# Batch 0 of a fused attention and mixer kernel: half of k by plain fp32 DMA and pooled on VectorE, all of q by casting DMA, and a new written order

## The chip, the cores and the metric

The kernel runs on one core of one Trainium2 chip. The metric is device time in microseconds (us). A time that differs by less than about 0.5% can't be told from no change here.

Names used: PE is TensorE, PEld its weight loads, DVE is VectorE, ACT is ScalarE, POOL is GpSimd, SP is SyncE. PSUM is what PE writes to.

## The reference, cut to what matters

Inputs are q, k and v of 8 batches x 8 heads x 576 rows x 64, fp32, and four weights. Eight neighbouring rows of k and v are averaged to 72 rows ("pooling"). Then attention, then a mixer over tokens and one over channels:

```python
k_p = k.reshape(B, H, 72, 8, D).mean(axis=3);  v_p = (same of v)
attn = softmax(q @ k_p.T / sqrt(D));  x = attn @ v_p        # x: batch, 576, 512
h  = relu(x.T @ w_tok1) @ w_tok2;     u = x + h.T           # over tokens, 576 -> 256 -> 576
h2 = relu(u @ w_ch1) @ w_ch2;         out = u + h2          # over channels, 512 -> 1536 -> 512
```

The device works in bf16 with fp32 sums.

## The kernel before, in words

**Stages.** A "unit" is the channel mixer of 512 rows: unit n for batch n, and a ninth unit for the last 64 rows of all batches. First come 12 tiles of layer 1 (`l1_tile`, L517, four matmuls of 512 columns each, evicted through a relu by ACT, L521), then the layer 2 products (`product`, L583), which use sums of activations and of weights that DVE makes (`g_sums`, L545 and L557, and `weight_sum`). While unit n runs, the attention and the token mixer of later batches are put between its matmuls.

**Attention of a batch b >= 1.** k and v come in by casting DMA (fp32 to bf16) from POOL's queue (`kv`, L118), q likewise (L128). k is pooled by three adds (`pool8`, L174, L175, L178/L180), on POOL as step K0/K1 or on DVE as k0/k1, or by identity matmuls on PE (`kpool`, L253). `kpT` transposes pooled k on PE. `qD` (Q0, Q1; L284) transposes q in 32 x 32 blocks on DVE, two heads packed per word. `scores` (s0, s1, s2; L297) makes the scores in the four row quadrants of PE, ACT takes the exponentials (L306). v is pooled on POOL (V0, V1), on DVE (v0, v1) or on PE (`ppool`, vpool0/1, L264). `av` (L379) multiplies by v, DVE divides (L383, L384). `at` (L393) and `u` (L415, L416) are the token mixer, `t` or a trip through DRAM transposes u for layer 1.

**Batch 0** has its own code before: two of four head pairs of q come as fp32 by SP's hardware queue (L738) and are cast by ACT and DVE (step c0, c1, L690), the others by casting DMA; q is transposed on PE (`qT`, L275, L277); k is pooled on PE in three pieces (`kp2`, L232, L234), transposed (`kt2`, L243, L246); scores are taken per head pair with odd and even rows apart (`score`, steps o, e; L318, L322); `avh` (a00 ... a14; L333, L338, L339), `ath` (m00 ...; L356), `uT_x`, `uT_a` (X, A; L468, L476, L478) carry on. Matmuls on zeros (d2, d3 ...; L679) stand before and between.

**What sets the order.** Nothing is scheduled by a planner when the kernel is built: the program order of each engine is the order in which the Python code runs. `HEAD` is the list of steps before unit 0. `PLAN[n]` gives for each half tile of unit n (index 0 to 44) the steps that follow it. Each engine works through its own list in order, and waits where its next instruction needs something. A "g" in the plan is `gate` (L712, L713): DVE writes a flag and POOL copies it, so that POOL's later work starts no earlier than that place in DVE's list. POOL's casting DMAs run one after another on one queue, and an issue waits while the eighth DMA before it has not landed.

PSUM: four banks for single tiles (p1a to p1d, `take`/`give`), and two double banks (p2, shown as p).

Of the kernel before, what the change touches and what calls it, by code (L numbers as in the profile page):

```python
# [8 lines left out]
FP32 = mybir.dt.float32  # L9
# [11 lines left out]
HEAD = """LkA LkT LkB LvT Lq LvA LvB Lt1 Lk1 Lt2 Lc1b Lc1a Lq1 Lc1c Lv1 Lc1d p1 Lc2a Lc2b Lc2c d2 d2 d3 d1 d4 d4 c0 c1 prep q0 kp0 kp1 kt0 q1 d1 o0 kt1 kp2 e0 e1 q3 kt2 o1 q2 e3 vpool0 o3 e2 a00 vpool1 a02 o2 m01 d1 d1 m00 a04 X1 m03 a14 m02 X0 m04 p0 a10 a12 1.kpool m10 m14 m12 m13 m11 A1 A0 X2 X3 A2 A3"""  # L21
PLAN = [
# [13 lines left out]
def kernel(  # L36
# [18 lines left out]
    BOUNCED = range(3, B)  # L55
    SP = S // POOL
    BP, BR = 64, S // 64
    NE = (BR + 1) // 2
    EV, OD = NE * BP, (BR - NE) * BP
# [37 lines left out]
    qf = area2[:, 0:4 * BR * D].bitcast(FP32).rearrange("p (a n) -> p a n", a=2)  # L97
# [89 lines left out]
    def batch_steps(b):  # L187
# [5 lines left out]
        def prepare():  # L193
            kp = att.tile([SP, 2, 2, 4, D // 2], BF16, name="kp") if b >= 1 else None
            st.update(kp=kp, vp=values[par], ex=exps[par], xt=rests[b // 2 % 2])
            if not first:
                st["kD"] = att.tile([P, 2, 2, SP], BF16, name="kD")
# [15 lines left out]
        def pool(eng, t, g):  # L213
            def go():
                hs = slice(g * HP, (g + 1) * HP)
                pool8(eng, loaded[b, t], hs, st["kp"][:, g] if t == "k" else st["vp"][:, hs, 0:D], t == "k")
            return go
# [9 lines left out]
        def kp2(h0, h1):  # L227
            def go():
                ps = take([P, 512], FP32)
                n = (h1 - h0) * D  # L230
                for i in range(POOL):
                    nc.tensor.matmul(out=ps[0:SP, 0:n], lhsT=ident[0:SP, 0:SP], rhs=loaded[b, "k"][:, h0:h1, i, :],  # L232
                                     start=(i == 0), stop=(i == POOL - 1))
                nc.vector.tensor_copy(out=kpz[:, h0:h1, 1, :], in_=ps[0:SP, 0:n].rearrange("j (h d) -> j h d", d=D))  # L234
                give(ps)
            return go

        def kt2(h0, h1):
            def go():
                ps = take([P, 2, h1 - h0, SP], BF16)  # L240
                for odd in range(2):
                    for h in range(h0, h1):
                        nc.tensor.transpose(out=ps[:, odd, h - h0, :],  # L243
                                            in_=kpz[:, h, 1 - odd:3 - odd].rearrange("j e d -> j (e d)"),
                                            identity=ident[0:SP, 0:SP])
                nc.vector.tensor_copy(out=kT[:, :, h0 * SP:h1 * SP], in_=ps.rearrange("m o h j -> m o (h j)"))  # L246
                give(ps)
            return go
# [22 lines left out]
        def qT(hp):  # L271
            def go():
                ps = take([P, NE, 2, BP], BF16)
                for rr in range(NE):
                    nc.tensor.transpose(out=ps[:, rr].rearrange("m l p -> m (l p)"),  # L275
                                        in_=loaded[b, "q"][:, hp, rr * P:(rr + 1) * P], identity=ident)
                nc.vector.tensor_copy(out=qT0[:, hp].rearrange("m l (r p) -> m r l p", p=BP), in_=ps)  # L277
                give(ps)
            return go

# [8 lines left out]
        def scores(i):  # L289
            def go():  # L290
                pss = [ps_two.tile([P, 2, 512], FP32, name="p2") for _ in range(2)]
                spans = [(i, 0, 0, S1)] if i < 2 else [(g, g * (S - S1), S1, S) for g in range(2)]
                for g, o, n0, n1 in spans:
                    for db in range(2):
                        for l in range(4):
                            quad = slice(l * 32, (l + 1) * 32)
                            nc.tensor.matmul(out=pss[l // 2][0:SP, l % 2, o:o + n1 - n0], lhsT=st["kD"][quad, g, db, :],  # L297
# [3 lines left out]
                for a in range(2):  # L301
                    if i < 2:
                        dst, src = exv[:, a, :, i, 0:S1], pss[a][0:SP, :, 0:S1]
                    else:
                        dst, src = exv[:, a, :, :, S1:S], pss[a][0:SP, :, 0:2 * (S - S1)].rearrange("j l (g n) -> j l g n", g=2)
                    nc.scalar.activation(out=dst, in_=src, func=AF.Exp, scale=scale)  # L306
            return go

        def score(hp, odd):
            n = OD if odd else EV  # L310

            def go():
                ps = ps_two.tile([P, 2, 512], FP32, name="p2")
                exv = st["ex"][:, 0:H * S].rearrange("j (h n) -> j h n", h=H)[:, 2 * hp:2 * hp + 2]
                for hl in range(2):
                    h = 2 * hp + hl
# [466 lines left out]
```

## Time and profile before

| what | us |
|---|---|
| median of 3 runs | 266.4 (266.19 to 267.63) |
| span of the profiled execution, its only time on the page | 264.4 |
| median less span | 2.0 |
| PE busy | 256.2 (97%) |
| DVE, ACT, POOL busy | 178.4, 119.6, 153.1 |
| first score matmul of batch 0 (L318) | at 9.74 |
| first product with v (L333) | at 15.16 |
| first layer 1 matmul (L517) | at 24.60 |

The page divides the span into 40 slices and gives each engine's busy share in tenths. The timeline gives the start, duration, engine, line and operation of each instruction, in order. "x8" is eight instructions in a row, whose duration is from the first's start to the last's end. A wait is put down to what ended it.

### The profile page before, as it was taken

How to read it: one execution, taken by the hardware profiler on the slowest of the kernel's cores; microseconds unless marked ns; L12 is line 12 of the kernel's file. 1: busy time of each engine (PE TensorE's matmuls, PEld its weight loads, DVE VectorE, ACT ScalarE, POOL GpSimd, SP SyncE). 2: the span in 40 equal slices, each digit the busy share in tenths (PEclk: the TensorE clock that was granted, in tenths of full speed). 3: DMA queues.
4: the chain of work that ended last, by engine and by line, in shares of the span. 5: the costliest groups of instructions: out<-in, count | busy, mean ns of one | idle time of the engine just before them, and what ended most of it. 6: DMA issues, size and time to landing. Idle time of an engine off the chain costs nothing.

```text
span 264.4 us, 5328 instructions
## 1 busy us (share of the span) xinstructions
PE 256.2 (97%) x2121; PEld 160.3 (61%) x2121; DVE 178.4 (67%) x370; ACT 119.6 (45%) x195; POOL 153.1 (58%) x177
## 2 busy tenths in 40 slices
PE   8799999989999999999999999999999999999994
PEld 3685466744677545774487447744874486486483
DVE  3557569996787655895599678844795576184183
ACT  2355763149536456425641575165435412612700
POOL 8577326899999999988959982898200010100000
PEclk9999999999999999999999999999999999999999
DMA  6999999993088928699447940830513053404104
GB/s 141 193 195 206 205 207 208 205 216 80 4 129 141 166 82 171 149 202 266 91 132 107 232 144 17 158 94 4 159 38 122 30 170 80 121 0 102 59 0 159
DMA packets 31704, 34.29 MB, mean 130 GB/s; under 512 B 3136, under 2 KB 23744, under 8 KB 31680
## 3 DMA queue, kind: packets, MB, share of 16 engines
q0 software_dynamic: 17632, 17.64, 42.3%
q1 hardware_dynamic: 13632, 15.93, 20.2%
q10 hardware_dynamic: 416, 0.39, 0.5%
q8 instruction: 16, 0.26, 0.4%
q14 instruction: 8, 0.07, 0.1%
HBM read 38.99 MB, written 12.58 MB: 195 GB/s over the span
## 4 chain that ended last, share of the span: by engine, by line
PE 73%; DVE 12%; POOL 8%; issue 3%; DMA 2%; ACT 1%; POOLq 0%; ACTq 0%
PE p1c L517 10%; PE p1b L517 8%; PE p1a L517 7%; PE p1d L517 7%; PE p1d L583 6%; PE p1c L583 5%; PE p1b L583 4%; PE p1a L583 4%; POOL t L174 3%; PE p L297 3%; DVE x L384 3%; DVE area L545 3%; PE p L379 2%; DMA kr<-in_k_dram 2%; POOL t L175 2%
## 5 line engine op out<-in xcount | busy, mean ns | idle before, releaser
L517 PEld LDWEIGHTS <-w_ch 128*128 128x128 bf16 x432 | 39.5, 98 | 44.4 <-issue 2.7
L713 POOL COPY flag<-flag 1x1 f32<-1x1 f32 x47 | 15.3, 326 | 86.0 <-DVE flag L712 86.0
L583 PEld LDWEIGHTS <-area 128*128 128x128 bf16 x432 | 41.4, 98 | 7.8 <-issue 1.2
L306 ACT ACTIVATE ex<-p 72x768 bf16<-72x768 f32 x42 | 31.6, 803 | 17.1 <-PE p L297 17.1
L583 PEld LDWEIGHTS <-GT 128*128 128x128 bf16 x324 | 30.7, 98 | 7.9 <-issue 1.6
L175 POOL TENSOR_TENSOR t<-t 72x512 f32<-72x512 f32 x23 | 31.2, 1358 | 1.8
L517 PE MATMUL p1c<-uT,w_ch 128*128 128x512 bf16 x116 | 31.4, 379 | 0.0
L521 ACT ACTIVATE GT<-p1b 128x512 bf16<-128x512 f32 x27 | 16.1, 597 | 27.5 <-PE p1b L517 20.9
L521 ACT ACTIVATE GT<-p1c 128x512 bf16<-128x512 f32 x32 | 19.1, 598 | 15.5 <-PE p1c L517 11.7
L517 PE MATMUL p1b<-uT,w_ch 128*128 128x512 bf16 x96 | 26.0, 379 | 0.0
L174 POOL TENSOR_TENSOR t<-kr 72x1024 f32<-72x1024 bf16 x12 | 25.5, 2121 | 0.4
L174 POOL TENSOR_TENSOR t<-vr 72x1024 f32<-72x1024 bf16 x11 | 23.4, 2125 | 1.0 <-DMA vr<-in_v_dram 0.5
L517 PE MATMUL p1a<-uT,w_ch 128*128 128x512 bf16 x88 | 23.9, 379 | 0.0
L517 PE MATMUL p1d<-uT,w_ch 128*128 128x512 bf16 x84 | 22.2, 379 | 0.0
L521 ACT ACTIVATE GT<-p1a 128x512 bf16<-128x512 f32 x25 | 14.9, 597 | 15.4 <-PE p1a L517 14.8
L521 ACT ACTIVATE GT<-p1d 128x512 bf16<-128x512 f32 x24 | 14.4, 599 | 12.8 <-PE p1d L517 7.3
L384 DVE TENSOR_TENSOR x<-p,den 128x512 bf16<-128x512 f32 x28 | 19.3, 691 | 1.0
L545 DVE TENSOR_TENSOR area<-GT 128x1536 bf16<-128x1536 bf16 x9 | 11.3, 1257 | 11.9 <-ACT GT L521 6.7
L557 DVE TENSOR_TENSOR area<-GT 128x1536 bf16<-128x1536 bf16 x9 | 9.5, 1054 | 11.3 <-ACT GT L521 11.3
L379 PEld LDWEIGHTS <-ex 72*128 72x128 bf16 x280 | 12.9, 98 | 6.5 <-DVE x L384 1.4
L379 PE MATMUL p<-vp,ex 72*128 72x65 bf16 x280 | 14.4, 194 | 0.3 <-POOL vp L180 0.2
L118 POOL DMA_DIRECT2D kr<-in_k_dram x17 | 10.9, 646 | 5.6 <-PE p1b L222 1.9
(185 smaller groups left out, 464.2 us busy)
## 6 DMA issues: line engine op xcount, KB each, us to landing
out_dram<-o SPq DMA_DIRECT2D x32, 256.0 KB, 4.2
qb<-in_q_dram POOLq DMA_DIRECT2D x7, 576.0 KB, 9.4
kr<-in_k_dram POOLq DMA_DIRECT2D x7, 512.0 KB, 8.4
vr<-in_v_dram POOLq DMA_DIRECT2D x7, 512.0 KB, 14.0
w_ch<-in_moe_w_ch_dram POOLq DMA_DIRECT2D x5, 512.0 KB, 14.8
mem<-u SPq DMA_DIRECT2D x10, 256.0 KB, 2.2
v<-mem SPq DMA_DIRECT2D x20, 128.0 KB, 2.9
area<-in_q_dram SPq DMA_DIRECT2D x2, 288.0 KB, 3.0
```

Source lines behind the costliest of these rows:

```text
L118: nc.gpsimd.dma_start(out=t[j0:j1, h0:h1].rearrange("j h i d -> j h (i d)"), in_=src[b, h0:h1].rearrange("h (j i) d -> j h (i d)", i=POOL) ...
L174: eng.tensor_tensor(out=t4[:, 0:n], in0=t[:, hs, 0:4], in1=t[:, hs, 4:8], op=ALU.add)
L175: eng.tensor_tensor(out=t4[:, 0:n, 0:2], in0=t4[:, 0:n, 0:2], in1=t4[:, 0:n, 2:4], op=ALU.add)
L306: nc.scalar.activation(out=dst, in_=src, func=AF.Exp, scale=scale)
L379: nc.tensor.matmul(out=ps[:, h // 4, (h % 4) * (D + 1):(h % 4 + 1) * (D + 1)], lhsT=st["ex"][:, h * S + n0:h * S + n0 + P], rhs=st["vp"][: ...
L384: nc.vector.tensor_tensor(out=dst.rearrange("p (a h d) -> p a h d", a=2, d=D), in0=view[:, :, :, 0:D], in1=den[rows, :, :, None].broadcast ...
L517: nc.tensor.matmul(out=ps, lhsT=w_ch1[:, kk, m * P:(m + 1) * P], rhs=uT[kk], start=(kk == 0), stop=(kk == 3))
L521: nc.scalar.activation(out=GT[:, m, :], in_=ps, func=AF.Relu)
L545: nc.vector.tensor_tensor(out=out, in0=a, in1=b, op=ALU.subtract)
L557: nc.vector.tensor_tensor(out=S4[:, 0], in0=GT[:, f, hi], in1=GT[:, sec, hi], op=ALU.add)
L583: nc.tensor.matmul(out=ps[i] if split else ps[:, i], lhsT=chunk(u, i, a(m)), rhs=w(m), start=start and m == 0 and (i == 0 or split), stop= ...
L713: nc.gpsimd.tensor_copy(out=flag[:, 1:2], in_=flag[:, 0:1])
```

## The change

- k of batch 0: heads 0 to 3 come as fp32 by the hardware queues (64 rows of the 72 from SP, 8 from ACT) into `kf`, and are pooled by three adds on DVE (step k0). Heads 4 to 7 come by casting DMA and are pooled on PE (kp1), as before but in one piece. Both are written in the layout of the other batches, transposed by two PE transposes each (`kt2`) and copied by DVE.
- q of batch 0: all by casting DMA, in two pieces of four heads, in the layout of the other batches, and transposed on DVE (Q0, Q1). `qT`, `score`, the casts c0 and c1 and the zero matmuls go. The scores are those of the other batches (s0, s1, s2).
- v of batch 0, heads 0 to 3: pooled on DVE (v0) where PE did it (vpool0); the same for batch 1. In later units four POOL steps become DVE steps: 5.K0, 6.K0, 7.V1 and 7.V0.
- `HEAD` and `PLAN` are written anew: order of the DMAs and of all steps, places of the gates. The pooling of batch 2's k loses the gate between its halves, and the transposes of that (2.kpT) go from index 44 of unit 0 to index 0 of unit 1. 0.u0 goes from unit 0 to the head.

```diff
-HEAD = """LkA LkT LkB LvT Lq LvA LvB Lt1 Lk1 Lt2 Lc1b Lc1a Lq1 Lc1c Lv1 Lc1d p1 Lc2a Lc2b Lc2c d2 d2 d3 d1 d4 d4 c0 c1 prep q0 kp0 kp1 kt0 q1 d1 o0 kt1 kp2 e0 e1 q3 kt2 o1 q2 e3 vpool0 o3 e2 a00 vpool1 a02 o2 m01 d1 d1 m00 a04 X1 m03 a14 m02 X0 m04 p0 a10 a12 1.kpool m10 m14 m12 m13 m11 A1 A0 X2 X3 A2 A3"""
+HEAD = """LkT LkB Lq0 LvT Lq+ LvA LvB Lt1 Lt2 Lk1 Lc1a prep Lq1 k0 Lc1b Lc1c Lv1 p1 kt0 Lc1d Lc2a Lc2b Q0 kp1 Q1 s0 kt1 s1 s2 v0 vpool1 Lc2c a00 a02 a04 p0 m01 a10 X0 X1 m02 a14 m04 m03 m00 a12 m14 m10 m11 A0 A1 m12 X3 m13 1.kpool X2 A3 A2 0.u0 1.Q1"""
-    {0: "2.lk 0.u1 1.kpT 1.Q0 1.Q1", 3: "0.u0 3.lq 2.lq", 6: "1.s0 0.u2", 8: "g", 9: "0.u3 1.s1", 10: "1.vpool1 2.lv", 12: "1.s2 1.vpool0", 13: "=3", 14: "1.av1 1.av2", 17: "1.av0", 18: "1.av4 g", 19: "w0", 20: "3.lv 1.av3", 22: "w1", 23: "g =1 =2", 24: "3.lk", 25: "=4", 26: "1.at0 g", 27: "2.K0", 28: "w3 1.at1", 30: "g", 31: "1.u2", 32: "2.K1", 33: "1.u0 2.V0", 34: "1.u1", 35: "w2", 37: "1.t2", 40: "1.u3", 41: "1.t0", 42: "1.t3", 43: "1.t1 2.Q0 1.u4", 44: "g 2.kpT 2.Q1 3.Q0"},
+    {0: "1.kpT g", 3: "2.lk", 4: "1.Q0 2.lq", 5: "1.s0", 6: "g", 7: "0.u2", 8: "1.v0 1.s1", 12: "1.s2", 13: "=3 1.vpool1 2.lv", 14: "3.lq g 3.lk 0.u1 1.av2", 16: "1.av1", 17: "1.av0 0.u3", 18: "1.av4", 20: "3.lv w0", 22: "1.av3 w1", 24: "1.at1", 25: "=1", 26: "=2", 27: "1.at0 =4", 28: "g 2.K0", 29: "2.K1", 30: "1.u0 g w3", 31: "1.u2", 33: "1.u1 2.V0", 34: "w2", 37: "1.t2", 39: "1.u3", 40: "1.t1", 42: "1.t0 2.Q0 1.t3", 43: "1.u4 2.Q1 g", 44: "3.Q0"},
...
+    kf = area[0:SP, 0:4096].bitcast(FP32).rearrange("j (l i d) -> j l i d", l=HP, i=POOL)
...
+        def kt2(g):
+            def go():
+                ps = take([P, 2, SP], BF16)
+                for e in range(2):
+                    nc.tensor.transpose(out=ps[:, e, :], in_=st["kp"][:, g, e].rearrange("j l d -> j (l d)"),
+                                        identity=ident[0:SP, 0:SP])
+                nc.vector.tensor_copy(out=st["kD"][:, g], in_=ps)
...
-    def late_q():
-        nc.gpsimd.dma_start(out=loaded[0, "q"][:, 2:HP, 0:BR * D], in_=q_pairs(2, HP))
+    def first_q(g):
+        if (0, "q") not in loaded:
+            loaded[0, "q"] = raw.tile([P, HP, BR * D + D], BF16, name="qb")
+        nc.gpsimd.dma_start(out=quarters(loaded[0, "q"])[:, g],
+                            in_=q[0, g * HP:(g + 1) * HP].rearrange("l (j n) d -> (l j) (n d)", n=2 * BR))
...
+        for j0, j1 in ((0, BP), (BP, SP)):
+            (nc.scalar if j0 else nc.sync).dma_start(out=kf[j0:j1].rearrange("j l i d -> j l (i d)"),
+                                                     in_=k[0, 0:HP].rearrange("h (j i) d -> j h (i d)", i=POOL)[j0:j1])
```

More of the change, by code (lines that the diff above doesn't have):

```diff
@@ L54 @@
     POOL = 8
-    BOUNCED = range(3, B)
+    BOUNCED = [b for b in range(B) if any(f"{b}.M" in t.split() for at in PLAN for t in at.values())]
     SP = S // POOL
     BP, BR = 64, S // 64
-    NE = (BR + 1) // 2
-    EV, OD = NE * BP, (BR - NE) * BP
     S1 = 3 * P
@@ L193, in prepare @@
         def prepare():
[L194 to L197, printed above, removed]
+            st["kp"] = att.tile([SP, 2, 2, 4, D // 2], BF16, name="kp")
+            st["kD"] = att.tile([P, 2, 2, SP], BF16, name="kD")
+            st.update(vp=values[par], ex=exps[par], xt=rests[b // 2 % 2])
         def late(key):
@@ L215, in go @@
                 hs = slice(g * HP, (g + 1) * HP)
-                pool8(eng, loaded[b, t], hs, st["kp"][:, g] if t == "k" else st["vp"][:, hs, 0:D], t == "k")
+                pool8(eng, kf if first and t == "k" else loaded[b, t], hs, st["kp"][:, g] if t == "k" else st["vp"][:, hs, 0:D], t == "k")
             return go
@@ L225, in kpT, with kp2 @@
             give(ps)
-        def kp2(h0, h1):
+        def kp2(g):
             def go():
                 ps = take([P, 512], FP32)
-                n = (h1 - h0) * D
+                hs = slice(g * HP, (g + 1) * HP)
                 for i in range(POOL):
-                    nc.tensor.matmul(out=ps[0:SP, 0:n], lhsT=ident[0:SP, 0:SP], rhs=loaded[b, "k"][:, h0:h1, i, :],
+                    nc.tensor.matmul(out=ps[0:SP, 0:HP * D], lhsT=ident[0:SP, 0:SP], rhs=loaded[b, "k"][:, hs, i, :],
                                      start=(i == 0), stop=(i == POOL - 1))
-                nc.vector.tensor_copy(out=kpz[:, h0:h1, 1, :], in_=ps[0:SP, 0:n].rearrange("j (h d) -> j h d", d=D))
+                nc.vector.tensor_copy(out=st["kp"][:, g].rearrange("j e l d -> j e (l d)"),
+                                      in_=ps[0:SP, 0:HP * D].rearrange("j (n e) -> j e n", e=2))
                 give(ps)
             return go
-        def kt2(h0, h1):
+        def kt2(g):
             def go():
[L240 to L246, printed above, removed]
+                ps = take([P, 2, SP], BF16)
[3 more added lines that the diff above has]
+                nc.vector.tensor_copy(out=st["kD"][:, g], in_=ps)
                 give(ps)
@@ L269, in ppool @@
             return go
[L271 to L279, printed above, removed]
         def qD(g):
@@ L287, in qD, with scores @@
             return go
-        def scores(i):
+        def scores(spans):
+            n = spans[0][2] - spans[0][1]
             def go():
                 pss = [ps_two.tile([P, 2, 512], FP32, name="p2") for _ in range(2)]
-                spans = [(i, 0, 0, S1)] if i < 2 else [(g, g * (S - S1), S1, S) for g in range(2)]
-                for g, o, n0, n1 in spans:
+                for i, (g, n0, n1) in enumerate(spans):
+                    o = i * n
                     for db in range(2):
@@ L296, in go @@
                             quad = slice(l * 32, (l + 1) * 32)
[L297 removed]
+                            nc.tensor.matmul(out=pss[l // 2][0:SP, l % 2, o:o + n], lhsT=st["kD"][quad, g, db, :],
                                              rhs=st["qD"][quad, g, n0:n1, db], start=(db == 0 and o == 0),
@@ L301, in go @@
                 for a in range(2):
-                    if i < 2:
-                        dst, src = exv[:, a, :, i, 0:S1], pss[a][0:SP, :, 0:S1]
+                    g, n0, n1 = spans[0]
+                    if len(spans) == 1:
+                        dst, src = exv[:, a, :, g, n0:n1], pss[a][0:SP, :, 0:n]
                     else:
-                        dst, src = exv[:, a, :, :, S1:S], pss[a][0:SP, :, 0:2 * (S - S1)].rearrange("j l (g n) -> j l g n", g=2)
+                        dst, src = exv[:, a, :, :, n0:n1], pss[a][0:SP, :, 0:2 * n].rearrange("j l (g n) -> j l g n", g=2)
                     nc.scalar.activation(out=dst, in_=src, func=AF.Exp, scale=scale)
[L307 to L316, printed above, removed]
-                    keys = slice(h * SP, (h + 1) * SP)
-                    nc.tensor.matmul(out=ps[0:SP, hl, 0:n], lhsT=kT[:, odd, keys], rhs=qT0[:, hp, hl, 0:n],
-                                     start=True, stop=True)
-                dst = exv.rearrange("j h (r p) -> j h r p", p=BP)[:, :, odd:BR:2, :]
-                src = ps[0:SP, :, 0:n].rearrange("j h (r p) -> j h r p", p=BP)
-                nc.scalar.activation(out=dst, in_=src, func=AF.Exp, scale=scale)
             return go
@@ L487, in batch_steps @@
                 name[t + str(g)] = pool(nc.vector, t, g)
-        for hp in range(HP):
-            if hp < 3:
-                hs = ((0, 2), (2, 4), (4, 8))[hp]
-                name[f"kp{hp}"], name[f"kt{hp}"] = kp2(*hs), kt2(*hs)
-            name[f"q{hp}"], name[f"o{hp}"], name[f"e{hp}"] = qT(hp), score(hp, 1), score(hp, 0)
-        for i in range(3):
-            name[f"s{i}"] = scores(i)
+        for g in range(2):
+            name[f"kp{g}"], name[f"kt{g}"] = kp2(g), kt2(g)
+            name[f"s{g}"], name[f"S{g}"], name[f"f{g}"] = (scores([(g, *r)]) for r in ((0, S1), (0, 512), (S1, S)))
+        name["s2"], name["S2"] = (scores([(g, n, S) for g in range(2)]) for n in (S1, 512))
         for c in range(5):
@@ L687, in head @@
             batches[1][0]()
-        elif s[0] == "c":
-            a = int(s[1:])
-            (nc.vector.tensor_copy if a % 2 else nc.scalar.copy)(out=loaded[0, "q"][:, a, 0:BR * D], in_=qf[:, a, :])
         else:
@@ L750 @@
             head(s)
-        for n in range(B + 1):
-            unit(n, PLAN[n])
+        for n, at in enumerate(PLAN):
+            unit(n, at)
 _INS = ['q', 'k', 'v', 'moe_w_tok1', 'moe_w_tok2', 'moe_w_ch1', 'moe_w_ch2']
```

15 lines of the change are left out of this document (2 added, 13 removed), and 16 rows, old and new, of the table PLAN.

## The prediction

> **What bounds the kernel now.** I read the page's busy line and slices first, then the busy time by stretches of 6 us, PE's waits, and the timeline of the head.
>
> ```profile
> PE 256.2 (97%) x2121; PEld 160.3 (61%) x2121; DVE 178.4 (67%) x370; ACT 119.6 (45%) x195; POOL 153.1 (58%) x177
> PE   8799999989999999999999999999999999999994
> POOL 8577326899999999988959982898200010100000
> ```
>
> PE is busy in nearly every slice after the fourth. POOL is full from slice 8 to about 20, then nearly idle. The stretches (columns: PE, PEld, DVE, ACT, POOL, then clock, DMA share, GB/s) say the same:
>
> ```profile
> 0.00:6.00 6.00, 4.81 (x15) 1.88 (x16) 2.51 (x11) 1.95 (x2) 4.89 (x13) 1.00 0.67 144
> 24.00:30.00 6.00, 6.00 (x38) 2.60 (x37) 3.72 (x7) 3.50 (x7) 1.29 (x2) 1.00 1.23 205
> 54.00:60.00 6.00, 5.08 (x47) 2.75 (x45) 5.54 (x10) 3.46 (x7) 5.69 (x5) 1.00 1.14 220
> 132.00:204.00 72.00, 71.80 (x632) 45.36 (x625) 54.19 (x117) 33.08 (x54) 43.45 (x46) 1.00 0.46 112
> ```
>
> From 24 us PE loses only 0.9 at 54 to 60, 0.3 at 84 to 96, 0.2 at 138 to 144 and the tail. PE's waits name the first two:
>
> ```profile
> PE p1c L222 <- POOL kp L178: 0.9, 1, 0.9
> PE p L379 <- POOL vp L180: 0.2, 1, 0.2
> ```
>
> So the time is: start of the first L517, plus PE's work from there (239.8 us with its waits). A change counts only as it moves that start, PE's later work, or a later PE wait. The head, from the timeline:
>
> ```profile
> 8.04 0.61 PE L232 MATMUL p1d<-kr,ident 72*72 72x128 bf16 x8 [1.30 <-DMA kr<-in_k_dram]
> 15.16 0.41 PE L333 MATMUL p<-vp,ex 72*128 72x65 bf16 x8 [0.41 <-ACT ex L322]
> 24.60 0.59 PE L517 MATMUL p1c<-uT,w_ch 128*128 128x512 bf16 x2
> ```
>
> PE waits for k's DMA, then for exponentials, and is full from 15.16 on.
>
> **A: PE's work after the first L517.** vpool0 of batch 1 goes: eight matmuls start at 34.65 and the next work at 35.55, so 0.9. 0.u0 moves ahead of it: 26.89 to 27.32, 0.4. Together -1.3. No other count on PE changes there.
>
> **B: the start of the first L517.** Landings of the old casting DMAs, from the DMA view narrowed to single issues, by KB queued in total: 256 at 6.65, 320 at 7.9, 576 at 9.3, 640 at 10.2, 928 at 11.25, 1184 at 12.65, 1440 at 13.9. The new queue holds kT, kB (288), q0 (576), vT (640), q+ (928), vA (1184), vB (1440): the same total beside the same fp32 bytes (576 KB by hardware, which landed by 4.3). So I take: kB 7.3, q0 9.3, q+ 11.25, vA 12.65, vB 13.9. The loads ahead of batch 1's v also sum to the same, so that lands at 31.5 as now. ACT issues one small DMA ahead of its table load (1.28 us): hidden, since its first exponential comes after 10.
>
> - k0 on DVE, from 4.3. Nearest rows are the three adds of 2.v1: 1.52, 1.64 and 0.84, 4.1 us from 59.21 to 63.29, beside a busy POOL. POOL only issues DMAs here. Low end: a DVE add from PSUM of 512 columns takes 0.68, so 1024, 512 and 256 columns are about 1.2, 0.65 and 0.4, 2.2 in all. k0 is done by 6.5 to 8.4, kt0 by 7.1 to 9.0. q0 covers either.
> - kp1: eight 256-column matmuls from 7.3, 0.9 (1.8 at half rate): hidden by q0 too.
> - Q0: 9.3 + 0.76 (row L284) = 10.05. s0 to its first exponential is 0.57 (28.71 to 29.28): 10.6. Two exponentials take 1.5: 12.1. Q1: 11.25 + 0.76 = 12.0; behind it in DVE's list stands kt1's copy, 0.3: 12.3. s1 0.57: 12.9 to 14.4. s2 about 0.45: 14.85 to 16.35.
> - v0 on DVE: 12.65 + 2.2 = 14.9, hidden (with 4.1, 16.75, 0.9 too late). vpool1 on PE: 14.9 to 15.8, and a00 follows at 15.8 where the product now starts at 15.16.
> - From a00 the division chain on DVE sets the pace: four at 0.9 and two at 0.6 from 16.3 reach 21.1. Then PE does m12, X3, m13 (0.22 each), 1.kpool 1.73, X2 0.22, A3, A2 and 0.u0 (0.43 each): 3.9. First L517 at 25.0, so +0.4. w_tok2 lands earlier (about 17 for 19.8) and is not in the way.
>
> **C: waits in unit 0.** v0 of batch 1 is new on DVE and waits for the landing at 31.5. Behind it stand =3 (0.9), vpool1's cast (0.35), u1 and the divisions. v0 ends at 33.8 (2.2; POOL again issues DMAs only) and the cast at 35.1. PE reaches av2 at 25.0 + 9.8 = 34.8: 15 half tiles of 0.432 are 6.5, and kpT, s0, u2, s1, s2, vpool1 and u1 are 3.3. A new wait of 0.3; with 4.1 for v0 it is 2.2.
>
> On goes DVE's list from 33.8: =3, the cast, three u and s of 0.65, five divisions of 0.9, w0, w1, =1, =2, =4 of 0.95: 12.4, the gate at 46.2. POOL's copy 0.8, then 2.K0 and 2.K1 of 4.35 each (47.87 to 52.2 now) without the flag of 0.9 between: 55.9. PE reached 2.kpT at 56.4 and now does at 56.4 + 0.4 + 0.3 - 1.3 + 0.4 (one index later) = 56.2. The wait of 0.9 goes, with 0.3 to spare: -0.9. POOL and PE are then both 1.6 ahead, so 3.K1 and batch 3's V meet PE as now.
>
> **D: four half poolings from POOL to DVE in units 3 to 5.** POOL's relief is worth nothing: no PE wait after 100 names it. DVE was busy 54.2 of 72 us there. Four times 2.2 fits in the idle 17.8; four times 4.1 just fills it. Low end 0, or -0.2 if a wait on DVE goes by the new order; high end 4 (below). PE lost only 0.2 where DVE was busy 5.8 of 6 (138 to 144), so I take +0.3.
>
> **Sum.** 264.4 - 1.3 + 0.4 + 0.3 - 0.9 + 0.3 = 263.2 of span. The median stood 2.0 above the span: 265.2.
>
> **The clock, row and rule.** The zero matmuls go, and with them what keeps PE busy early:
>
> ```profile
> 2.87 1.49 PE L679 MATMUL p1c<-area 128*128 128x512 bf16 x3
> 4.57 1.03 PE L679 MATMUL p1a<-area 128*128 128x512 bf16 x4
> ```
>
> Three take 1.49 (0.43 apart), later four take 1.03 (0.217 apart): half rate until 4.5, after 3.3 us of unbroken matmuls. Now PE starts near 7 with 1.8 us of kp1, then short pieces with gaps until 14.9. The trace has no row for that. I take full rate by s1.
>
> The Trainium skill, "TensorE: Matmul & The Clock Gate", section "Part 1: The HAM clock gate", says that half rate is the default and that about 3.4 us of sustained matmuls lift it; this trace's rows agree. Read strictly it would give the first rival's time.
>
> **Rivals.**
>
> 1. *Half rate lasts into the a-steps.* For it: no 3.3 us stretch before 14.9. Against: PE was broken up from 6.9 to 8.0 too and stayed fast. s0, s1 and s2 cost about 0.25 each, vpool1 1.8 for 0.9: a00 at 17.4. The 4.3 us of PE work up to m12 has 5.2 of division chain as cover; with 3 us of it at half rate it is 5.8, so +0.5. First L517 at 27.1: 264.4 + 2.5 - 1.3 - 0.9 + 0.3 (C's new wait gone, PE being late) = 265.0, so 267.0.
> 2. *DVE becomes the bound in units 3 to 5* (slower than before). Place: the eviction of u, or a division, behind 5.k0, 6.k0, 7.v1, 7.v0. Each holds DVE for up to 4.1; PE has other PSUM banks for three tiles of 0.87, 2.6. From there on PE waits: 1.5 for each of the first two, and with 7.v1 and 7.v0 close together (=3 between) 1 more: 263.2 - 0.3 + 4 = 266.9, so 268.9. For it: 4.1 is the only row of DVE pooling. Against: POOL was busy only 1.2 of the 26 us from 186, so the last two run alone and would be near 2.2.
>
> The Trainium skill, "GPSIMD Engine Reference", section "1. Specifications", says that the two engines share SBUF interfaces, with contention at DVE instructions of two SBUF inputs, as these adds are. The 1.64 of row L175, against 0.65 by columns, agrees.
>
> 3. *More waits go.* Batch 3's V (0.2), the three waits on divisions (0.2, 0.2, 0.4) and the tail's on s (0.3) end too, and D costs nothing: 262.9 - 1.2 = 261.7, so 263.7. For it: =3 is moved ahead in the last unit, POOL has less to do. Against: those on DVE are of one engine that gets more work.
>
> **How the numbers follow.** Chances: forecast 0.45, clock 0.25, DVE 0.17, more waits gone 0.13. The forecast's own range is 264.3 to 266.3 (v0's price and D). The range of 8 in 10 takes in the clock rival, the third, and the DVE rival where it costs up to 3 of its 4: 263.5 to 268.0. With the bounds of 0.5% at 265.07 and 267.73: faster 0.22 + 0.04 + 0 + 0.13 = 0.39; slower 0.02 + 0.04 + 0.12 = 0.18; same 0.43.
>
> **What would show it.** B: first L481 (the new line of L517) at 25.0, a00's product (L300) at 15.8, Q0 at 9.3. A row of 0.43 apart for 512 columns, or 0.213 for 256, after 12 us speaks for rival 1. C: av2's first product (new L345) waiting for vp about 0.3, and no PE wait for POOL's kp near 56. D: new PE waits for DVE between 130 and 215. What would make it wrong: q0's DMA not keeping the place in the queue that its bytes give it; 64 KB on eight partitions took 1.25 us before, and half of that now stands first.

## The result: 4.8% slower

The kernel after takes 279.14 us (median of four, 277.15 to 281.17), the kernel before 266.29 beside it: a ratio of 1.048, 95% interval 1.042 to 1.053. Forecast were 265.2 and a range up to 268.0. The profiled execution has a span of 277.1 (before 264.4), so 12.7 us are to be found.

The busy line and the slices of the page, after:

```profile
PE 252.6 (91%) x2029; PEld 156.8 (57%) x2054; DVE 196.6 (71%) x375; ACT 118.0 (43%) x192; POOL 133.6 (48%) x159
PE   0679999999978999999699899999999999999994
POOL 8592342599994999949829900592010100000000
PEclk9999999999999999999799999999999999999999
```

PE's share fell from 97% to 91%. It does nothing in the first slice, and there are dips in slices 12, 13, 20 and 23. The clock row has one new mark, a 7 in slice 20 (131.6 to 138.6 us). The busy time by the stretches that were shown of before, and one more (PE, PEld, DVE, ACT, POOL, clock, DMA share, GB/s):

```profile
0.00:6.00 6.00, 0.00 (x0) 0.00 (x0) 1.25 (x9) 1.28 (x1) 4.79 (x13) 1.00 0.71 135
24.00:30.00 6.00, 5.78 (x36) 3.45 (x36) 2.91 (x6) 1.60 (x4) 0.00 (x0) 1.00 1.24 204
54.00:60.00 6.00, 5.51 (x55) 4.39 (x53) 5.74 (x10) 1.22 (x3) 5.76 (x4) 1.00 0.56 90
132.00:138.00 6.00, 3.26 (x13) 0.92 (x11) 3.99 (x5) 1.12 (x3) 5.68 (x5) 0.72 0.29 46
132.00:204.00 72.00, 67.12 (x551) 40.40 (x555) 56.38 (x108) 31.97 (x53) 33.71 (x34) 0.98 0.46 102
```

Between 132 and 204 us PE lost 0.2 before and loses 4.9 now. PE's waits after (us in total, count, longest):

```profile
PE p1a L234 <- DVE kp L170: 8.4, 1, 8.4
PE p1c L382 <- DVE o L590: 2.0, 1, 2.0
PE p1b L213 <- DVE kp L170: 1.7, 1, 1.7
PE p1d L481 <- DVE uT L425: 1.3, 1, 1.3
PE p1a L382 <- DVE u L383: 1.0, 1, 1.0
PE p1b L213 <- POOL kp L170: 0.7, 1, 0.7
```

The first is only the start of PE's work. The wait of 0.9 for POOL's kp at the end of unit 0 is gone, as forecast; the last line is that of batch 3, at 76.8. Four waits of 1 to 2 us are new, all on DVE. The head, from the timeline of PE after:

```profile
8.51 1.90 PE L223 MATMUL p1b<-kr,ident 72*72 72x256 bf16 x8
15.71 1.92 PE L254 MATMUL p1d<-vr,ident 72*72 72x256 bf16 x8
17.43 1.09 PE L300 MATMUL p<-vp,ex 72*128 72x65 bf16 x16
29.91 0.59 PE L481 MATMUL p1b<-uT,w_ch 128*128 128x512 bf16 x2
```

Eight matmuls of 256 columns take 1.90 and 1.92, where v's took 1.04 before:

```profile
13.23 1.04 PE L264 MATMUL p1b<-vr,ident 72*72 72x256 bf16 x8
```

So PE runs at half rate, and by the spacing of all matmuls it does so until 25.35. The clock column says 1.00 for these stretches, so it can't be used there; the spacing of equal matmuls can. Layer 1 begins at 29.91, 5.3 later than before.

The other 7.4 lie behind it. Largest are the waits of 2.0 at 84.4, 1.75 and 0.99 at 134 to 135, and 1.3 at 157.8, and 3.4 us of half rate right behind those at 134 (134.58 to 137.99), worth 1.7. Here is DVE, then POOL, at the place of the first and of the second wait (start, duration):

```profile
79.18 2.61 DVE L509 TENSOR_TENSOR area<-area,GT 128x1536 bf16<-128x1536 bf16 x1
81.82 1.90 DVE L509 TENSOR_TENSOR area<-GT,area 128x1536 bf16<-128x1536 bf16 x1
127.88 3.58 DVE L166 TENSOR_TENSOR t<-kr 72x1024 f32<-72x1024 bf16 x1
131.50 1.64 DVE L167 TENSOR_TENSOR t<-t 72x512 f32<-72x512 f32 x1
133.17 0.83 DVE L170 TENSOR_TENSOR kp<-t 72x256 bf16<-72x256 f32 x1
```

```profile
78.82 2.15 POOL L166 TENSOR_TENSOR t<-vr 72x1024 f32<-72x1024 bf16 x1
81.04 1.87 POOL L167 TENSOR_TENSOR t<-t 72x512 f32<-72x512 f32 x1
128.24 2.14 POOL L166 TENSOR_TENSOR t<-vr 72x1024 f32<-72x1024 bf16 x1
130.45 2.13 POOL L167 TENSOR_TENSOR t<-t 72x512 f32<-72x512 f32 x1
132.66 1.05 POOL L172 TENSOR_TENSOR vp<-t 72x256 bf16<-72x256 f32 x1
```

The first of these two waits is for a bank that DVE empties (`o`, L590) behind the last two activation sums of unit 1 (steps =2 and =4). They take 2.61 and 1.90 beside POOL's pooling of batch 3's v (3.V1). Before, that pooling came after them, and they took 0.95 each:

```profile
73.04 0.95 DVE L545 TENSOR_TENSOR area<-area,GT 128x1536 bf16<-128x1536 bf16 x1
75.17 0.95 DVE L545 TENSOR_TENSOR area<-GT,area 128x1536 bf16<-128x1536 bf16 x1 [0.57 <-DVE s L626]
77.36 2.15 POOL L174 TENSOR_TENSOR t<-vr 72x1024 f32<-72x1024 bf16 x1
```

The step moved to DVE, 5.k0, takes 6.0 us beside POOL's 5.V0. The sum of what is named behind the start of layer 1, with A's -1.3 taken as forecast, is -1.3 - 0.9 (C) + 2.0 (unit 1) + 2.7 (5.k0) + 1.7 (half rate behind it) + 1.3 (at 157.8) + 0.7 (batch 3's kp) = 6.2 of 7.4. The rest is in pieces below 0.6.

### The profile page after: what moved, and what is told of

It reads as the page before. It is cut to its first block, busy times and chain, and to the rows that moved or that the text cites. A ratio compares the mean times of both kernels' runs of the same rounds, so it can differ in the third digit from the quotient of the medians.

```text
span 277.1 us, 5151 instructions
## 1 busy us (share of the span) xinstructions
PE 252.6 (91%) x2029; PEld 156.8 (57%) x2054; DVE 196.6 (71%) x375; ACT 118.0 (43%) x192; POOL 133.6 (48%) x159
## 4 chain that ended last, share of the span: by engine, by line
PE 62%; DVE 15%; POOL 9%; issue 8%; ACT 2%; DMA 2%; POOLq 0%; DVEq 0%; ACTq 0%
PE p1d L481 7%; PE p1c L481 7%; PE p1a L481 6%; PE p1d L547 5%; PE p1b L547 5%; PE p1b L481 4%; PE p1c L547 4%; PE p1a L547 4%; POOL t L166 4%; DVE area L509 4%; PE p L279 3%; POOL t L167 3%; DMA area<-in_k_dram 2%; DVE t L166 2%; PE p L346 2%
## 5 line engine op out<-in xcount | busy, mean ns | idle before, releaser
L677 POOL COPY flag<-flag 1x1 f32<-1x1 f32 x41 | 9.9, 241 | 125.3 <-DVE flag L676 125.3
L289 ACT ACTIVATE ex<-p 72x768 bf16<-72x768 f32 x48 | 36.1, 803 | 28.9 <-PE p L279 28.9
L481 PE MATMUL p1d<-uT,w_ch 128*128 128x512 bf16 x103 | 29.0, 389 | 1.6 <-DVE uT L425 1.3
L481 PE MATMUL p1c<-uT,w_ch 128*128 128x512 bf16 x99 | 27.3, 379 | 0.2
L166 POOL TENSOR_TENSOR t<-kr 72x1024 f32<-72x1024 bf16 x10 | 21.8, 2182 | 0.3
L481 PE MATMUL p1b<-uT,w_ch 128*128 128x512 bf16 x73 | 20.0, 379 | 0.1
L166 POOL TENSOR_TENSOR t<-vr 72x1024 f32<-72x1024 bf16 x9 | 19.2, 2136 | 0.4
L521 DVE TENSOR_TENSOR area<-GT 128x1536 bf16<-128x1536 bf16 x9 | 9.3, 1035 | 13.3 <-ACT GT L485 13.2
L279 PE MATMUL p<-qD,kD 32*72 32x384 bf16 (+1 forms) x256 | 14.7, 312 | 1.7 <-ACT ex L289 1.7
L547 PE MATMUL p1c<-area,area 128*128 128x256 bf16 x96 | 12.8, 272 | 0.1
```

What stands on the lines that cost most here:

```text
L166: eng.tensor_tensor(out=t4[:, 0:n], in0=t[:, hs, 0:4], in1=t[:, hs, 4:8], op=ALU.add)
L279: nc.tensor.matmul(out=pss[l // 2][0:SP, l % 2, o:o + n], lhsT=st["kD"][quad, g, db, :], rhs=st["qD"][quad, g, n0:n1, db], start=(db == 0 ...
L481: nc.tensor.matmul(out=ps, lhsT=w_ch1[:, kk, m * P:(m + 1) * P], rhs=uT[kk], start=(kk == 0), stop=(kk == 3))
L521: nc.vector.tensor_tensor(out=S4[:, 0], in0=GT[:, f, hi], in1=GT[:, sec, hi], op=ALU.add)
L547: nc.tensor.matmul(out=ps[i] if split else ps[:, i], lhsT=chunk(u, i, a(m)), rhs=w(m), start=start and m == 0 and (i == 0 or split), stop= ...
L677: nc.gpsimd.tensor_copy(out=flag[:, 1:2], in_=flag[:, 0:1])
```

## The experiments

Theory: the head loses by half rate on PE, since nothing keeps PE busy without gaps; the plan loses where POOL's and DVE's adds meet, and by half rate that the resulting PE waits bring on. Rivals: the new head's chain of engines is late anyway; DVE has too much work as a whole, wherever its steps stand; waits are worth their own length and the clock is a side effect. Spans are of profiled executions; where a ratio is given, the kernel ran in three rounds beside the kernel before. The others were executed once. The four executions of the kernel after have spans of 275.3 to 279.4, so a difference of a few us between single spans counts here only where the traces name what makes it.

### Head and plan apart

`head_new_plan_old`: the kernel after with the plan of before; `head_old_plan_new`: the kernel before with the plan of after.

```diff
@@ HEAD of head_new_plan_old (its PLAN is that of before)
-X2 A3 A2 0.u0 1.Q1
+X2 A3 A2
@@ HEAD of head_old_plan_new (its PLAN is that of after)
-A1 A0 X2 X3 A2 A3
+A1 A0 X2 X3 A2 A3 0.u0 1.Q1
```

> The new head (without its last two steps, which the old plan has itself) with the old plan of all units. Theory (the loss is 5.3 in the head and 7.4 in the plan): layer 1 starts at 29.5, the units lose about 3 us of PE waits as before, span 264.4 + 4.9 = 269.3. Rival (the plan's losses come from the late head): the old plan shows new PE waits of 5 us and more, span above 273.

> The old head (with 0.u0 and 1.Q1 behind it, which the new plan expects there) and the new plan of all units. Theory (5.3 in the head, 7.4 in the plan): layer 1 starts at 25.0 and the waits near 84, 134 and 158 stay, shifted by 5: span 277.1 - 4.9 = 272.2. Rival (the plan's losses come from the late head): the waits go and the span is 263 to 265.

New head alone: span 269.4, layer 1 at 29.54, waits of the units as before. New plan alone: span 274.9, layer 1 at 24.76, and PE's waits on DVE of 2.0, 1.7, 1.0 and 1.2 again. So the head costs 5.0, as expected, and the plan 10.5, not the 7.8 expected: two stretches of half rate follow its waits here, 79.92 to 83.34 and 131.12 to 137.95, together 10.2 us or 5.1 of time. In the kernel after, the first of them did not come, and the second was half as long.

### The head: zero matmuls in, and out

`warm`: zero matmuls put into the new head. `old_no_zeros`: all taken out of the old one.

```diff
@@ HEAD of warm
-Lc1a prep
+Lc1a d4 d4 d4 d4 prep
...
-Q0 kp1 Q1 s0 kt1 s1 s2
+Q0 kp1 d2 Q1 s0 kt1 d2 s1 d2 s2
@@ HEAD of old_no_zeros
-Lc2c d2 d2 d3 d1 d4 d4 c0
+Lc2c c0
...
-q1 d1 o0
+q1 o0
...
-m01 d1 d1 m00
+m01 m00
```

> The changed kernel with zero matmuls put back into its head (16 before k0, two after each of kp1, kt1 and s1). Theory clock: half rate lasted to 25.4 us because PE had no unbroken stretch of matmuls; with them it ends near 4.5, 256-column pooling matmuls stand 0.11 apart, a00 starts near 16.0 and layer 1 near 25.5 instead of 29.9, and the span is 277.1 - 4.4 = 272.7 (time about 274.7). Rival, the head is late by its loads and exponentials: the clock is full but layer 1 still starts after 28 and the span stays above 275.

> The kernel before with the sixteen zero matmuls ahead of its pooling and the three behind it taken out, nothing else changed. Theory (the zeros are what lifts TensorE to full rate): matmuls stay at half rate until about 25 us, the first layer-1 matmul comes at 28.5 to 30 us where it came at 24.6, the span is 4 to 5.5 us longer than 264.4, time about 270.5 us. Rival (the old head would warm up by its own steady matmuls; only the new head's order keeps TensorE at half rate): full rate by 10 us, first layer-1 matmul at 24.0 to 25.0, span 264 to 265, time about 266.

With the zeros layer 1 of the new head begins at 25.09, where the forecast had 25.0, so the chain of engines was costed rightly and the first rival falls. The span is 274.0 (272.7 expected), only 3.1 less: half rate came at 80.74 to 84.16 as well, behind the same wait of 2.0, which is worth 1.7.

The second run hit neither expectation: span 266.4, layer 1 at 26.34, 1.7 late. From its timeline of PE:

```profile
10.11 1.90 PE L232 MATMUL p1c<-kr,ident 72*72 72x256 bf16 x8
15.00 1.04 PE L264 MATMUL p1c<-vr,ident 72*72 72x256 bf16 x8
26.34 0.59 PE L517 MATMUL p1b<-uT,w_ch 128*128 128x512 bf16 x2
```

The old head starts at half rate too without zeros, but is at full rate by 15.0. One thing that differs is how densely PE works. Its busy time in old_no_zeros, then in the kernel after:

```profile
8.00:14.00 6.00, 6.00 (x49) 5.17 (x48) 2.37 (x7) 1.88 (x3) 3.42 (x6) 1.00 1.27 194
```

```profile
8.00:16.00 8.00, 5.86 (x46) 3.06 (x47) 4.85 (x9) 3.33 (x5) 5.69 (x9) 1.00 1.25 202
16.00:26.00 10.00, 9.09 (x75) 6.90 (x75) 4.82 (x13) 3.29 (x5) 5.89 (x8) 1.00 1.26 205
```

Six us at 100% were enough to lift the rate; 73% and 91%, in pieces, did not until 25.35. The busy share alone is not the measure, though. In the kernel after PE was busy 3.40 of the 3.42 us from 15.11 to 18.53, and the rate stayed at half; it rose behind 134.58 to 137.99 with 2.64 of 3.41. The matmuls of the first stretch use 32 or 72 rows of PE's array; those of the second, like the zeros, use 128. Gaps and rows were not varied apart, so which of them counts for how much is open. Zeros are worth 1.7 us in the old head and 4.8 in the new, which has less work of its own for PE.

`warm_plan_old` is warm with the old plan; `dense_plan_old` has more zeros:

```diff
@@ HEAD of dense_plan_old, against warm_plan_old
-Lc1a d4 d4 d4 d4 prep
+Lc1a d4 d4 d4 d4 d4 d4 prep
...
-kp1 d2 Q1 s0 kt1 d2 s1 d2 s2 v0 vpool1 Lc2c a00 a02 a04
+kp1 d4 Q1 s0 kt1 d4 s1 d4 s2 d2 v0 vpool1 Lc2c a00 d2 a02 d1 a04
```

> The kernel after with its zero matmuls back in the new head (sixteen of N 512 ahead of the pooling, two behind kp1, kt1 and s1 each) and the old plan for all units, 0.u0 and 1.Q1 back in unit 0. Theory (the head loses by its clock alone, the plan loses by the rest): first layer-1 matmul at 24.7 to 25.2, PE waits of the units as before, no half-rate stretch behind 30 us, span 264.4 to 265, time 266.0 to 266.8, ratio within 0.5% of 1. Rival (the new head costs the units something too, by the order in which it leaves the DVE and POOL queues): first layer-1 matmul as said, span 267 or more, time 269 or more.

> The kernel after with the old plan for all units (0.u0 and 1.Q1 back in unit 0) and more zero matmuls in its head than the run with sixteen plus six: twenty-four ahead of the pooling, four each behind kp1, kt1 and s1, two behind s2, two and one between the first a-steps, so that TensorE is not half idle between 10 and 17 us. Theory (the gate falls back to half rate where waits leave TensorE too little to do, 15.4 to 22 us in the run with fewer zeros; filled waits hold full rate): full rate from 5 us on in all executions, first layer-1 matmul at 25.0 to 25.6 where it was 27.87, span 264.4 to 265.6 where it was 268.0, time 266.2 to 267.4. Rival (the new head has work missing at 15 to 22 us for another reason, such as contention of DVE and POOL): first layer-1 matmul at 27 or later, span 267 or more, time 269 or more.

warm_plan_old: 269.71 us, ratio 1.011 (1.008 to 1.014), neither what the theory nor quite what the rival gave. Its stretches show why, PE and clock above all:

```profile
12.00:14.00 2.00, 1.21 (x11) 0.37 (x11) 1.46 (x3) 1.54 (x3) 1.26 (x2) 1.00 1.33 196
14.00:16.00 2.00, 1.37 (x20) 1.03 (x20) 1.63 (x3) 1.45 (x3) 1.23 (x3) 0.87 1.30 198
16.00:18.00 2.00, 2.00 (x23) 1.76 (x21) 0.20 (x1) 1.61 (x4) 2.00 (x4) 0.50 1.23 206
20.00:22.00 2.00, 2.00 (x22) 1.77 (x20) 1.15 (x4) 0.00 (x0) 1.50 (x3) 0.50 1.20 213
```

PE is busy 60 to 70% from 12 to 16 us with no wait above 0.8, and the rate fell to half until about 22. The same head kept its rate in warm, so this is at the edge. Layer 1 came at 27.87. (One of the four executions has a mean clock of 1.000 and, with 267.7, about the span of the others; since the clock column misses half rate at the start, it proves nothing by itself.) dense_plan_old, whose fillers lie in those waits, has spans of 265.4 to 266.8 in all eight executions, at clocks of 0.998 to 1.000: layer 1 at 25.74, span 265.8 in the profiled one, 267.59 us, ratio 1.005 (1.003 to 1.008). Each is a little above what the theory gave (25.6, 265.6, 267.4). So 3.6 of the head's 5.0 are the clock. The 1.4 that stay are layer 1's start 1.1 later and 0.3 behind it.

### The plan: taking apart DVE and POOL

`k0_gate`: a gate behind 5.k0, so that POOL's 5.V0 starts after it. `k0_pool`: 5.k0 back on POOL.

```diff
@@ PLAN[3] of k0_gate
-10: "5.k0 4.at0 5.Q1"
+10: "5.k0 g 4.at0 5.Q1"
@@ PLAN[3] of k0_pool
-10: "5.k0 4.at0 5.Q1"
+10: "5.K0 4.at0 5.Q1"
```

> The changed kernel with one gate more, behind 5.k0, so that POOL's next pooling (5.V0) starts when DVE's is done. Theory contention: 5.k0 takes 6.0 us because POOL pools beside it; alone it takes 2.3 to 2.8, PE's waits of 1.75 and 1.0 near 134 go, and with them the half-rate stretch of 3.4 us that follows (1.7 us): span 277.1 - 4.5 = 272.6. Rival, DVE has simply too much in its list there: 5.k0 gets shorter but PE still waits over 1.5 for kp or u, and the gain is under 1.5.

> The kernel after with one step put back on its old engine: batch 5's k half 0 pooled on POOL (4.2 us there) at the same place of the plan. Head and clock there as in the kernel after. Theory (5.k0 on DVE beside POOL's 5.V0 is what costs): the waits of 1.75 for kp and 1.0 for u near 134 and the half-rate stretch behind them go; kp is there at about 132.6; span 272.5 to 274, time about 275. Rival (POOL then is the bound in unit 3, as 5.V0 and 5.V1 come 4.3 us later): waits for POOL's kp or vp of 2 us or more between 132 and 150, span 276 to 279, time about 279.

k0_gate, from the timeline of DVE:

```profile
127.97 1.18 DVE L166 TENSOR_TENSOR t<-kr 72x1024 f32<-72x1024 bf16 x1
129.18 0.69 DVE L167 TENSOR_TENSOR t<-t 72x512 f32<-72x512 f32 x1
129.90 0.42 DVE L170 TENSOR_TENSOR kp<-t 72x256 bf16<-72x256 f32 x1
```

The same three adds take 2.3, not 6.0. The waits at 134 and the half rate behind them are gone, span 273.5: 3.6 of 4.5 expected, as a wait for DVE's x near 147 grew by 0.9 (1.3 for 0.4). No work was taken from DVE, so it is the place and not the amount.

k0_pool: span 275.6, between the two expectations. The waits at 134 went, but POOL's batch 5 pooling now ran later, into DVE's next sum, and PE's waits show a new pair:

```profile
PE p1c L382 <- DVE o L590: 2.0, 1, 2.0
PE p L346 <- DVE x L351: 1.8, 1, 1.8
PE p L346 <- POOL vp L172: 1.4, 1, 1.4
```

The meeting was only moved: a sum took 3.24 from 145.38 on. 3.4 us of half rate came as well, behind the wait of 2.0 at 83 (mean clock 0.89 from 76 to 92). Of the 1.5 by which the span is shorter, 1.2 is the head's, which in this execution began layer 1 at 28.71.

`old_head_gates`: old head, new plan, with the gate of k0_gate and one behind the last activation sum of unit 1 (=4, which the expectations call the third weight sum), so that 3.V1 follows the sums. `warm_gates`: the same two gates with warm's head.

```diff
@@ PLAN[1], PLAN[3]
-27: "=2", 28: "=4", 29: "2.at1"
+27: "=2", 28: "=4 g", 29: "2.at1"
-10: "5.k0 4.at0 5.Q1"
+10: "5.k0 g 4.at0 5.Q1"
```

> The old head with the new plan (span 274.9 with two half-rate stretches) and the two gates: one behind 5.k0, one behind the third weight sum of unit 1, so that POOL pools after DVE's work at these places and not beside it. Theory (the plan loses 10.5 us by 2.0 and 2.7 of waits that contention of DVE and POOL makes, and by the half rate behind them, 10.2 us of it worth 5.1): both waits and both stretches go, span 264.5 to 266.5, time 266.3 to 268.3, clock 0.997 or above. Rival (the plan leaves too little slack for its poolings, so that moving them makes new waits): waits of 1.3 for DVE's x and 1.1 for uT near 141 and 148 grow to 3 or more together, half-rate stretches stay, span 268 or more, time 270 or more.

> The kernel after with the same zero matmuls in its head, a gate behind 5.k0, and a gate behind the third weight sum of unit 1, so that POOL pools 3.v half 1 after DVE's sums and not beside them. Theory (two poolings that run beside DVE's work cost 2.0 us at the wait for the sum's bank and 2.7 at the waits for 5.k0 and u, and each brings a half-rate stretch worth 1.7): the sums of unit 1 take 0.95 each, both waits and both stretches go, TensorE stays at full rate from 6 us on, span 265.5 to 267, time 267 to 268.7. Rival (the later poolings become the wait: 3.av and 5.av then wait for POOL's vp): waits on POOL vp of 2 us or more, span 269 to 274, time 271 to 276.

old_head_gates: span 266.0, 268.10 us, ratio 1.007 (1.004 to 1.009), clock 0.997 to 1.000 in all five executions. From its timeline of DVE, and its waits of PE:

```profile
74.38 0.95 DVE L545 TENSOR_TENSOR area<-area,GT 128x1536 bf16<-128x1536 bf16 x1
75.37 0.96 DVE L545 TENSOR_TENSOR area<-GT,area 128x1536 bf16<-128x1536 bf16 x1
```

```profile
PE p L379 <- DVE x L384: 1.3, 1, 1.3
PE p1c L517 <- DVE uT L458: 0.7, 1, 0.7
```

The sums are back at 0.95, and two gates recover 8.9 of the plan's 10.5. warm_gates missed its mark: 272.00 us, ratio 1.018 (1.013 to 1.024), four executions with spans of 267.8, 269.4, 270.6 and 270.7 at clocks of 0.990, 0.985, 0.979 and 0.974. In the one with a trace both waits are gone, so the gates did their part; the rate fell in its head (17 to 20 us), as in warm_plan_old. Why the other three are longer no trace shows.

`old_head_filled`: head_old_plan_new, nothing moved, with matmuls of no use in three of its waits.

```diff
@@ PLAN[1], PLAN[3], unit
-31: "2.u3"
+31: "f8 2.u3"
-15: "5.kpT 4.u1"
+15: "f7 5.kpT f4 4.u1"
...
+elif s[0] == "f":
+    ps = ps_two.tile([P, 2, 512], FP32, name="p2")
+    for _ in range(int(s[1:])):
+        nc.tensor.matmul(out=ps[:, 0], lhsT=ident, rhs=w_ch1[:, 0, 0:512], start=True, stop=True)
```

> The old head with the new plan, nothing moved, and matmuls whose result is not read put on TensorE into three of its waits: eight ahead of 2.u3, seven ahead of 5.kpT, four ahead of 4.u1 (4.0 us of work at full rate into 4.7 us of waits). Theory (a wait of 2 to 3 us makes the gate fall back to half rate for 3.4 us and more): the waits stay by the other engines' times, the half-rate stretches behind 79 and 131 us go, clock 0.997 or above in all executions, span 269 to 270.5, time 270.8 to 272.3. Rival (the stretches have another cause than the idle of TensorE): clock 0.98 to 0.99 as without the fillers, span 274 to 276, time 276 to 278.

From its timeline of PE:

```profile
77.41 1.89 PE L728 MATMUL p<-w_ch,ident 128*128 128x512 bf16 x7
79.56 0.59 PE L415 MATMUL p1d<-AT,w_tok 128*128 128x512 bf16 x2 [0.27 <-DVE o L626]
```

Work that nobody needs made the kernel 4.1 us faster: span 270.8, where the one execution of head_old_plan_new had 274.9, with PE reaching L415 at 79.56 as against 79.37. The half rate worth 5.1 is gone: the clock is 1.0 in all four executions (0.981 without the fillers). 273.07 us, ratio 1.026 (1.023 to 1.029), a little above the 272.3 expected. The rival that the clock is a side effect falls: the idle of PE lowers the rate, and the rate costs time of its own.

### All three mends, and two edits on the old kernel

`all_mended` is the kernel after with the head of dense_plan_old and both gates.

> The kernel after with all three mends together: the denser zero matmuls of its head, the gate behind 5.k0, and the gate behind the third weight sum of unit 1. It leaves 0.u0 and 1.Q1 in the head, as the kernel after has them. Theory (the 12.7 us are the half rate of the head, two contended pieces of DVE work, and the half rate behind their waits, and nothing else of size): the head costs 1.4 us as with the old plan, the gated plan 1.6 as with the old head, so span 264.4 + 3.0 = 267.4, give or take 1, time 268.2 to 270.2, clock 0.997 or above. Rival (new head and new plan also cost together, by what the head leaves late for unit 0 or by half rate that the plan's other waits bring): span 269.5 or more, time 271.3 or more, or a clock of 0.99 or less.

271.10 us, ratio 1.017 (1.014 to 1.021), span 269.7 (268.6 to 269.7 in four), clock 0.998 to 1.000: above what the theory gave, and at the rival's lower edge. The mends recover 7.4 of 12.7. Behind the head's first zeros there is no half rate left. Against the two halves (1.4 and 1.6) it is 2.3 more in the profiled execution, 1.2 in the fastest. The trace names about as much: layer 1 at 26.72 where dense_plan_old had 25.74, and two waits for the transposes of u that go through DRAM, 1.2 each at 149 and 226 (old_head_gates: one, of 0.7). Of the 1.0 in the head, 0.4 is 0.u0, moved there. The rest comes from the start: the zeros ran at half rate until 6.89 (3.82 in dense_plan_old), and PE came to its first transposes of k at 9.18 (8.37). Why the transfers for u land late was not tried.

`old_two_edits`: two of the change's edits alone on the kernel before.

```diff
@@ PLAN[0]
-10: "1.vpool1 2.lv", 12: "1.s2 1.vpool0"
+10: "1.v0 1.vpool1 2.lv", 12: "1.s2"
-28: "w3 1.at1", 30: "g", 31: "1.u2"
+28: "w3 1.at1", 31: "1.u2"
```

> The kernel before with two small edits: batch 1's v half 0 pooled on DVE right as it lands (1.v0 ahead of 1.vpool1) in place of eight matmuls and a copy, and the gate between the two poolings of batch 2's k on POOL taken out. Theory (TensorE is the bound, so each step's work or wait that goes is worth its own length): -0.9 for the matmuls of the vpool and -0.9 for the wait of 2.kpT, span 262.6, ratio 0.993 to 0.995. Rival (a pooling started earlier runs beside DVE's work and costs there what it saves): a new wait of 0.5 or more between 31 and 60 us, ratio 0.998 to 1.005.

266.37 us, ratio 0.999 (0.996 to 1.002): no gain, as the rival had it, though not by a new wait of 0.5 or more: the old one stayed. PE's wait and the adds on POOL before it:

```profile
56.94 0.24 PE L222 MATMUL p1b<-ident,kp 72*128 72x72 bf16 x2 [1.08 <-POOL kp L178]
```

```profile
50.77 1.66 POOL L178 TENSOR_TENSOR kp<-t 72x256 bf16<-72x256 f32 x1
52.50 2.13 POOL L174 TENSOR_TENSOR t<-kr 72x1024 f32<-72x1024 bf16 x1
```

The flag (0.9) between the halves of 2.k is gone, but POOL's last add of the first half took 1.66 where it took 0.84. It met a weight sum of DVE's that began at 50.77 too and took 0.94. In the kernel before the same two met at 51.4, and there POOL's add took 0.84 and DVE's sum 1.62. So the second half began only 0.57 earlier than before. PE came there 0.72 earlier (55.86 for 56.58) and waited 1.08, where it had waited 0.92.

No version here is faster than the kernel before.

## Why the prediction was wrong

**What bounds the kernel, and A.** PE was the bound, and the sum by start of layer 1, PE's work and PE's waits was the right frame. The -1.3 of A could not be seen by itself after. In old_two_edits the same vpool edit brought PE past 2.kpT 0.56 earlier, and 0.29 of that was there already at the start of layer 1, so at most 0.3 of the 0.9 is seen. Work taken from PE ahead of a wait for POOL counts only as far as POOL gets earlier too, and A did not make that condition.

**B failed at "I take full rate by s1".** What stands ahead of it was near: k0 took 2.4 (taken 2.2), though from 5.95 and not 4.3, q0 landed at 8.3 (9.3), and with the rate held (warm) layer 1 came at 25.1 (25.0). That this last is so close is in part luck: there the first product with v came at 15.32 (15.8), and the way from it took 0.6 longer than forecast. But half rate lasted to 25.35, and layer 1 came at 29.9: +5.3 for +0.4. The argument against rival 1, that the old kernel's PE was broken up from 6.9 to 8.0 and stayed fast, was about keeping a rate, for one us, not about gaining it through seventeen. Rival 1 had the mechanism and priced it at 2.5, since it let half rate end with the first a-steps. The Trainium skill, "TensorE: Matmul & The Clock Gate", section "Part 1: The HAM clock gate", asks for a busy window of about 3.4 us. The traces agree in the main: full rate came after 3.3 us unbroken in the kernel before (2.6 in dense_plan_old, 5.7 in all_mended), and in the kernel after not for 17 us of mostly broken work. Unbroken work is not enough by itself there, as the stretch from 15.11 to 18.53 shows. The rule that the prediction quoted and did not follow was the better guide than the row it preferred.

**C was right for the wait at 56, and too wide behind it.** The wait for POOL's kp went, 0.9, and av2 does not wait for v0. In the kernel after both PE and POOL are over 5 us late there; head_old_plan_new, where they are not, shows it too: POOL's kp was done at 56.48, and PE came at 56.98 without a wait. The rest of the new order is needed for that, since old_two_edits, with the gate out of the old order, kept the wait. But "3.K1 and batch 3's V meet PE as now" failed for 3.K1: its kp is a new wait of 0.7, behind an add on POOL of 1.43 (0.84 alone) that met a sum of DVE's. Two sums of the prediction are off by a little: 2.K1's end adds up to 55.7, not 55.9, and the waits of rival 3 to 1.3, not 1.2.

**D failed as the term of +0.3.** A half pooling on DVE costs 2.3 when POOL is quiet: 6.k0, 7.v1 and 7.v0 did, and cost nothing seen on PE, so DVE's total was no bound. 5.k0 stood beside POOL's 5.V0 and took 6.0, above the bound of 4.1, since that came from a row only partly covered: PE waited 2.7, and 1.7 of half rate followed. Rival 2 had the place (the eviction of u behind 5.k0), and priced this meeting at 1.5 where it cost 4.4.

**On no list** were two things. First, unit 1: the steps there were not moved to another engine, but 3.V1 was moved by the order onto the activation sums, +2.0. The prediction asked which DVE steps were new, not which of POOL's adds now stood beside which of DVE's. Second, that a wait can bring half rate: 1.7 in the profiled execution, 5.1 in head_old_plan_new.

## What to carry to other kernels

Before taking out filler matmuls, or work that PE did on the way, look for the densest stretch that remains: a head that kept PE 60 to 70% busy in pieces, with matmuls of 32 and 72 rows, stayed at half rate or could fall back to it here, and a wait of 2 us in mid-kernel could cost its length and 1.7 more. When poolings are moved between DVE and POOL, or only reordered, list for each add with two SBUF operands what the other engine does at that time; the totals of busy time say nothing of it, and a gate in the right place was worth more here (8.9 us for two) than any step moved. Read the rate from the spacing of equal matmuls where the clock column has not yet changed.

## What the runs showed of the hardware

- DVE and POOL take turns by whole instructions. DVE's add at 79.18 took 2.61: POOL's add from 78.82 ended at 80.97, and 0.95, the sum's own time, from there gives 81.92 (it ended at 81.79). POOL's next, 1.27 alone, took 1.87 and DVE's next 1.90. The Trainium skill, "SBUF — State Buffer", section "Who interferes with whom", says that a DVE instruction with two SBUF inputs contends with a GpSimd instruction that reads SBUF, for ports that are an exclusive lock, and that issue order decides who blocks. The trace agrees on the lock, to about 0.15 us: the price of a meeting is the rest of the other's instruction, up to 2.4 us for an add here, not a factor. On who blocks it is less clear: DVE's add at 127.88 is recorded 0.36 before POOL's and ended as if it had come second (128.24 + 2.14 + 1.22 = 131.60, seen 131.46).
- Half rate came in mid-kernel behind idle shorter than the stretch it caused: after 2.0 us of wait, 3.4 us of half rate (head_old_plan_new, warm), and in the kernel after not at all behind the same wait at 84.4. The times at which the rate changes give a reason that fits every case here, though none of them was set by an experiment. Within each trace they lie whole multiples of 3.413 us apart: 25.35, 134.58 and 137.99 in the kernel after (32 and 1), and 79.92, 83.34, 131.12 and 137.95 in head_old_plan_new (1, 14 and 2). Cut the traces into stretches by that grid, and the wait of 2.0 lies within one stretch in head_old_plan_new (76.51 to 79.92, PE busy 42% of it), warm (41%) and k0_pool (42%), and the rate fell at its end each time. In the kernel after and in k0_gate a border falls into the wait, both stretches are 68 to 72% busy, and the rate stayed. Between 28 and 250 us every stretch at full rate that was busy up to 45% was followed by half rate, and none from 59% up; in the heads, with matmuls of fewer rows, 60 and 72% were (warm_plan_old, warm_gates). Where the grid lies differs between executions.
- The executions of one kernel differ in the same direction as their clock: the four of the kernel after have spans of 275.3, 277.1, 277.7 and 279.4 at mean clocks of 0.997, 0.994, 0.992 and 0.986.
- The trace of the kernel after lacks some 25 matmul records, so its count of matmuls was not used.
